# Eight batches of memory attention and routed experts on one core: loads of the first queries ahead of the keys, gate weights from GpSimd's queue, the first quarter of w1 by groups, and a new table of places

## The chip, the cores and the metric

One core of a Trainium2 chip runs the whole program. The metric is device microseconds from the start to the end of one execution. Three runs of the kernel before gave a median of 415.57 us. A separate execution was recorded by the hardware profiler; all rows below come from that one.

## What is computed

```python
# memory attention, per batch (8) and head (8); seq 576, head_dim 64, 32 memories
a = exp(phi - max(phi, axis=2)); a = a / (sum(a, axis=2) + 1e-9)      # over the 576 tokens
k_m = einsum('bhsm,bhsd->bhmd', a, k); v_m = einsum('bhsm,bhsd->bhmd', a, v)
attn = softmax(q @ k_m.T / sqrt(64)); x = attn @ v_m                  # -> (8, 576, 512)
# routed experts: 8 experts, w1 512x1024, w2 1024x512
logits = x @ w_gate; local = sigmoid(x @ w_local)
for each batch, for each token in order:
    e = argmax(logits) if first token or local < 0.5 else the token before's e
    out = softmax(logits)[e] * (relu(x @ w1[e]) @ w2[e])
```

The main part of the kernel computes, for each batch, the expert of its first token for all tokens and scales by the gate where that is the token's expert; other pairs of batch and expert that occur are added by a loop at the end (`rest`).

## The kernel before, in words

The work goes batch by batch. Per batch there are these pieces, each a function that the table `PLACES` names:

- *Memories.* `phi`, `k` and `v` are loaded (`fetch_phi`, `fetch_kv`; lines 226 to 243). The maximum over tokens is taken and spread (`f_colmax`, `f_pm`, `f_mc`, `f_pm2`, `f_cx`), subtracted, and the exponential taken (`f_sub`, `f_exp`). `f_asum` adds over tokens, `f_pkv` (line 389) is 72 small matrix products of phi with keys and values (144 instructions in the trace), in batch 0 in two pieces, of six token groups and of three; `f_sums` gives the denominators, `f_rinv` and `f_kvn` normalise, `f_pT` and `f_kvT` transpose.
- *Gate.* `f_pgg` (line 448) multiplies the memories with the gate weights `wg`, `f_ggt` copies the result to the buffer `ggt`.
- *Attention in two halves of 288 tokens*, a and z: transposed queries (`k_qT`; in batch 0 `k_q0`, products with the identity on TensorE), scores (`k_psc`), then on VectorE and ScalarE `k_turn`, `k_mx`, `k_sub`, `k_exp`, `k_sum`, `k_inv`, `k_mul`, `k_at`. The values are not multiplied in: w1 is multiplied with the memories' values instead (`w_pg`, quarter or half of the 1024 columns at a time, and `w_G`), so that G stands for w1. G and the attention are split into a high part in fp32r and the rest (`k_ah`, `k_al`; Gh, Gl).
- *The expert of the first token.* `c_pl` (line 575) gives its logits, `c_choice` (line 586) the index on VectorE, `expert` reads it into a register of SyncE. Only then can SyncE issue the loads of w1 and w2 (`load1`, `load2`), whose addresses depend on it.
- *The expert's products.* `hidden` (line 804): for tokens 0 to 255 four pairs of 128-column chunks, then for tokens 256 to 575 eight chunks, six matrix products for each chunk (Gh and Gl with the high attention, Gh with the low), evicted by ScalarE (Relu to fp32r) and VectorE (the rest). `w_split` splits w2 (ScalarE, then GpSimd). `second` and `second_turned` multiply with w2.
- *Gate of all tokens.* The `g_` steps, short VectorE instructions.

Order: `start` (line 1145) writes out by hand the head of batch 0 and parts of batch 1. Then `moe` runs batch by batch as a generator; each `yield` adds its estimated TensorE time to a clock, and every step whose place in `PLACES` is not above that clock is emitted there. A step is known by its name and its batch; a batch is 37.8 units long. The order of emission is the order on each engine's queue and on SyncE's DMA queue, where all loads and stores of this kernel stand. `warm(n)` issues n products of zeros that nothing reads.

In batch 0, tokens are handled in three blocks (`EARLY`): the first 32 tokens alone, so that the choice of the expert can be made, then 32 to 287, then 288 to 575. `fetch_q0` is a generator: its first part loads the first 32 queries (`q0e`, line 270), its second the rest (`q`, line 291, and again line 270). In `start` it is called behind the four loads of keys and values of batch 0; between its two parts stand phi of batch 1 and the two loads of gate weights (lines 190 and 191). `w_pg` for the first quarter of w1 is called as `lo`, for the second as `hi`, both in `start`, before the first product of `hidden`.

PSUM buffers: `ps_a` 3, `ps_h` 3 (hidden, quarter products, query transposes), `ps_o` 2.

## Time and profile before

| what | us |
|---|---|
| median of three runs | 415.57 |
| lowest and highest run | 414.13, 419.14 |
| profiled execution, whole | 420.2 |
| its span, first to last instruction | 418.3 |
| TensorE busy in the span | 396.8 |
| VectorE, ScalarE, GpSimd busy | 284.6, 177.8, 149.1 |

Times in the rows are microseconds from the start of the span. PE is TensorE's matrix products, PEld its weight loads, DVE VectorE, ACT ScalarE, POOL GpSimd, SP SyncE; SPq is SyncE's queue, where an entry's length is the time in which it was issued, not that of the transfer. In a timeline a row has its start, its length, the engine, the line, the operation, the tile written and read, the shape and the count; in brackets stands the idle time of the engine before it and what ended it. "issue" there means that the profile shows nothing that was waited for. The share of the DMA engines can stand a little above 1, since it counts packets that overlap.

### The profile page before, as it was taken

Reading aid. Unit: us, or ns where it says so; the run is one execution under the profiler, and the core shown is the slowest. Engines: PE = TensorE matmul, PEld = TensorE weight load, DVE = VectorE, ACT = ScalarE, POOL = GpSimd, SP = SyncE. Lnnn points to the kernel's source line nnn. Section 1 sums busy time; section 2 is a strip of 40 time slices with the busy share of each in tenths; the row PEclk is TensorE's granted clock in tenths of the full one; section 3 lists DMA queues with packets and bytes.
Section 4 is the critical chain, followed back from the end, with each engine's and each line's share of the span. In section 5 each row is a group of like instructions: output and inputs, shape, how many; then the busy total and the mean of one; then the engine's idle time right before and its main releaser. Section 6 shows DMA issues by size and latency. Waiting matters only on the chain.

```text
span 418.3 us, 10597 instructions
## 1 busy us (share of the span) xinstructions
PE 396.8 (95%) x4191; PEld 328.0 (78%) x4195; DVE 284.6 (68%) x714; ACT 177.8 (43%) x427; POOL 149.1 (36%) x160
## 2 busy tenths in 40 slices
PE   8678789999999989999999999999999999999994
PEld 2546667889787887699868997798878996899884
DVE  4476586787978698687758868588757676626300
ACT  2154633336641664525632474426541564146010
POOL 1014541426522555018610481119510670256000
PEclk9999989999999999999999999999999999999998
DMA  8879693999188966799979179884974077202011
GB/s 257 208 260 292 124 393 99 233 266 384 38 284 147 327 226 214 121 356 323 300 132 394 68 258 184 241 303 140 253 145 164 2 220 257 99 0 64 25 40 54
DMA packets 116437, 82.58 MB, mean 197 GB/s; under 512 B 70624, under 2 KB 90080, under 8 KB 116384
## 3 DMA queue, kind: packets, MB, share of 16 engines
q1 hardware_dynamic: 116384, 81.86, 66.1%
q8 instruction: 35, 0.57, 0.6%
q14 instruction: 18, 0.15, 0.1%
HBM read 66.60 MB, written 15.24 MB: 196 GB/s over the span
## 4 chain that ended last, share of the span: by engine, by line
PE 82%; DMA 6%; DVE 5%; SPq 4%; issue 1%; ACT 1%; POOL 0%; DVEq 0%
PE ph L819 20%; PE po L907 9%; PE po L857 9%; PE po L909 8%; PE po L908 8%; PE po L859 8%; PE po L858 8%; PE pkv L396 4%; PE pg L787 3%; DMA kv_t<-in_v_dram 3%; DMA out_dram<-oT 2%; PE psc L507 2%; DVE h L829 1%; DMA q<-in_q_dram 1%; PE pl L604 1%
## 5 line engine op out<-in xcount | busy, mean ns | idle before, releaser
L777 POOL TENSOR_TENSOR w2l<-raw,w2h 128x512 fp32r<-128x512 f32 x64 | 82.0, 1305 | 32.7 <-ACT w2h L776 25.1
L819 PE MATMUL ph<-ah,Gh 128*128 128x256 f32 (+1 forms) x256 | 74.5, 306 | 3.0 <-issue 1.7
L829 DVE SCALAR_TENSOR_TENSOR h<-ph,h 128x320 fp32r<-128x320 f32 (+2 forms) x104 | 52.7, 519 | 33.6 <-ACT h L827 33.2
L819 PE MATMUL ph<-ah,Gl 128*128 128x256 f32 (+1 forms) x256 | 71.7, 295 | 0.0
L907 PE MATMUL po<-h,w2l 128*128 128x320 f32 x224 | 71.5, 319 | 0.0
L909 PE MATMUL po<-h,w2h 128*128 128x320 f32 x224 | 69.2, 309 | 0.0
L908 PE MATMUL po<-h,w2h 128*128 128x320 f32 x224 | 69.2, 309 | 0.0
L827 ACT ACTIVATE h<-ph 128x320 fp32r<-128x320 f32 (+1 forms) x96 | 46.5, 490 | 46.2 <-PE ph L819 45.9
L857 PE MATMUL po<-w2h,h 128*128 128x512 f32 (+1 forms) x152 | 61.2, 403 | 0.0
L914 POOL TENSOR_TENSOR oT<-oT,gT 128x320 f32<-128x320 f32 x28 | 20.9, 745 | 106.3 <-DVE oT L913 99.4
L859 PE MATMUL po<-w2h,h 128*128 128x512 f32 (+1 forms) x152 | 58.5, 385 | 0.0
L858 PE MATMUL po<-w2l,h 128*128 128x512 f32 (+1 forms) x152 | 58.4, 384 | 0.0
L819 PEld LDWEIGHTS ph<-ah,Gh 128*128 128x128 f32 x256 | 48.1, 188 | 9.2 <-issue 5.6
L819 PE MATMUL ph<-al,Gh 128*128 128x256 f32 (+1 forms) x256 | 54.6, 295 | 0.0
L819 PEld LDWEIGHTS ph<-ah,Gl 128*128 128x128 f32 x256 | 48.2, 188 | 0.0
L907 PEld LDWEIGHTS po<-h,w2l 128*128 128x128 f32 x224 | 42.0, 188 | 5.6 <-issue 5.2
L563 POOL TENSOR_TENSOR al<-at,ah 128x576 fp32r<-128x576 f32 (+1 forms) x18 | 23.1, 1291 | 63.9 <-ACT ah L559 54.2
L776 ACT ACTIVATE w2h<-raw 128x512 fp32r<-128x512 f32 x64 | 38.3, 624 | 11.9 <-PE po L909 10.1
L908 PEld LDWEIGHTS po<-h,w2h 128*128 128x128 f32 x224 | 42.1, 188 | 0.2
L909 PEld LDWEIGHTS po<-h,w2h 128*128 128x128 f32 x224 | 42.1, 188 | 0.0
L819 PEld LDWEIGHTS ph<-al,Gh 128*128 128x128 f32 x256 | 41.0, 188 | 0.0
L857 PEld LDWEIGHTS po<-w2h,h 128*128 128x128 f32 x152 | 29.0, 191 | 14.5 <-issue 9.4
(151 smaller groups left out, 578.0 us busy)
## 6 DMA issues: line engine op xcount, KB each, us to landing
raw<-in_moe_w_dram SPq DMA_DIRECT2D x34, 512.0 KB, 5.9
raw<-in_moe_w_dram SPq DMA_DIRECT2D x15, 1024.0 KB, 5.9
kv_t<-in_k_dram SPq DMA_DIRECT2D x7, 1152.0 KB, 8.9
kv_t<-in_v_dram SPq DMA_DIRECT2D x7, 1152.0 KB, 11.3
q_t<-in_q_dram SPq DMA_DIRECT2D x112, 72.0 KB, 3.4
att_d<-at SPq DMA_DIRECT2D x8, 576.0 KB, 9.0
out_dram<-oT SPq DMA_DIRECT2D x28, 160.0 KB, 5.7
out_dram<-ot SPq DMA_DIRECT2D x17, 256.0 KB, 4.8
```

The source lines that it names most:

```text
L563: (eng or nc.gpsimd).tensor_tensor(out=st.al[:, gs, ss], in0=st.at[:, gs, ss], in1=st.ah[:, gs, ss], op=ALU.subtract)
L776: nc.scalar.activation(h, src, AF.Copy)
L777: nc.gpsimd.tensor_tensor(out=l, in0=src, in1=h, op=ALU.subtract)
L819: nc.tensor.matmul(pv[:, c - c0], lhsT=lt[:, g, cs], rhs=rt[:, g, s0 : s0 + n], start=(i == 0), stop=(i == 5),)
L827: nc.scalar.activation(hc[:, :, 0:n], pv, AF.Relu)
L829: nc.vector.scalar_tensor_tensor(out=hc[:, :, o : o + z - a], in0=pv[:, :, a:z], scalar=0.0, in1=hc[:, :, a:z], op0=ALU.max, op1=ALU.subtract,
L857: nc.tensor.matmul(po[:, c0:c1], lhsT=h[:, c, th], rhs=hi, start=(c == 0), stop=False)
L858: nc.tensor.matmul(po[:, c0:c1], lhsT=h[:, c, th], rhs=lo, start=False, stop=False)
L859: nc.tensor.matmul(po[:, c0:c1], lhsT=h[:, c, tl], rhs=hi, start=False, stop=(c == FC - 1))
L907: nc.tensor.matmul(po[:, 0:n], lhsT=lo, rhs=h[:, c, 0:n], start=(c == 0), stop=False)
L908: nc.tensor.matmul(po[:, 0:n], lhsT=hi, rhs=h[:, c, 0:n], start=False, stop=False)
L909: nc.tensor.matmul(po[:, 0:n], lhsT=hi, rhs=h[:, c, n : 2 * n], start=False, stop=(c == FC - 1))
```

## The change

In words: the first part of `fetch_q0` is called ahead of the loads of keys and values, the gate weights are issued by GpSimd, ahead of GpSimd's constants, and the rest of the queries right behind phi of batch 1. The transposes of the first 32 queries stand ahead of `f_pkv`. The warm-up of three products that stood between `f_pm` and `c_pl` stands ahead of the transposes of the second block. The values of batch 1 and the first half of w2 are named in the table instead of `start`; so are the product with the second quarter of w1 and its split, now behind the first pair of hidden chunks. The first quarter is split group by group, with the attention's high part of the same group behind it, and the first pair of hidden chunks has a PSUM buffer for each chunk and does its products with the low part last. The column sums of batch 1 move from `start` to the table, and `pkv` is three steps there. Many numbers of the table differ; the rows of it that are named in the text, and those that are new, are shown.

```diff
--- PLACES, in part
+++
-    "asum": {2: 31, 3: 64.8, 4: 92.7, 5: 128.3, 6: 165.5, 7: 203.9},
-    "pkv": {1: 1.56, 2: 34.5, 3: 67.3, 4: 93.6, 5: 128.9, 6: 166.7, 7: 204.5},
+    "v": {1: 0.02},
+    "asum": {1: 1.42, 2: 31, 3: 64.8, 4: 92.7, 5: 128.3, 6: 165.5, 7: 203.9},
+    "pkv 0": {1: 1.56, 2: 33.9, 3: 67.3, 4: 93.6, 5: 128.9, 6: 166.7, 7: 204.5},
+    "pkv 1": {1: 1.57, 2: 34.51, 3: 67.31, 4: 93.61, 5: 128.91, 6: 166.71, 7: 204.51},
+    "pkv 2": {1: 1.58, 2: 34.52, 3: 67.32, 4: 93.62, 5: 128.92, 6: 166.72, 7: 204.52},
-    "kvn": {1: 7.7, 2: 36.8, 3: 70.1, 4: 95.5, 5: 131.7, 6: 170, 7: 208.2},
+    "kvn": {1: 8.6, 2: 36.8, 3: 70.1, 4: 96.1, 5: 131.7, 6: 170, 7: 208.2},
-    "z sub": {0: 0.01, 1: 26.1, 2: 54.9, 3: 90, 4: 123, 5: 162.6, 6: 198.6, 7: 240.9},
+    "z sub": {0: 1.21, 1: 26.1, 2: 54.9, 3: 90, 4: 123, 5: 162.6, 6: 198.6, 7: 240.9},
-    "w2 0": {1: 22.7, 2: 57.9, 3: 93.2, 4: 121.1, 5: 161.2, 6: 199, 7: 235.9},
-    "pg 0": {1: 30.7, 2: 66.7, 3: 96.2, 4: 127.7, 5: 165.8, 6: 203.6, 7: 240.5},
-    "G 0": {1: 30.8, 2: 66.8, 3: 96.9, 4: 129.9, 5: 167.7, 6: 205.2, 7: 242.1},
-    "g L": {0: 6.9, 1: 30.9, 2: 62, 3: 95.2, 4: 133.4, 5: 171.2, 6: 209, 7: 248.2},
+    "w2 0": {0: 0.93, 1: 22.7, 2: 57.9, 3: 93.2, 4: 124.1, 5: 164.2, 6: 202, 7: 238.9},
+    "pg 0": {0: 0, 1: 30.7, 2: 66.7, 3: 96.2, 4: 127.7, 5: 165.8, 6: 203.6, 7: 241.1},
+    "G 0": {0: 0.01, 1: 30.8, 2: 66.8, 3: 96.9, 4: 129.9, 5: 167.7, 6: 205.2, 7: 242.7},
+    "g L": {0: 7.6, 1: 30.9, 2: 62, 3: 96.4, 4: 133.4, 5: 171.2, 6: 209, 7: 248.2},
...
@@ -187,8 +190,8 @@
             nc.gpsimd.memset(c0s[i], 0.0)
 
     def gate_weights():
-        nc.sync.dma_start(out=wg[:, :, 0:E], in_=w_gate.rearrange("(h p) e -> p h e", h=HG))
-        nc.sync.dma_start(out=wg[:, :, E : E + 1], in_=w_local.rearrange("(h p) o -> p h o", h=HG))
+        nc.gpsimd.dma_start(out=wg[:, :, 0:E], in_=w_gate.rearrange("(h p) e -> p h e", h=HG))
+        nc.gpsimd.dma_start(out=wg[:, :, E : E + 1], in_=w_local.rearrange("(h p) o -> p h o", h=HG))
 
     def pair_constants():
         nc.gpsimd.iota(pos, pattern=[[32, 2]], base=1, channel_multiplier=1, allow_small_or_imprecise_dtypes=True)
@@ -554,9 +557,9 @@
         ss = slice(32 * p[1], 32 * p[2])
         nc.vector.transpose(st.at[:, :, ss], st.sc[p[1]].rearrange("p (g i) m -> p g (i m)", g=NG))
 
-    def k_ah(st, b0, b1):
+    def k_ah(st, b0, b1, gs=slice(0, NG)):
         ss = slice(32 * b0, 32 * b1)
-        nc.scalar.activation(st.ah[:, :, ss], st.at[:, :, ss], AF.Copy)
+        nc.scalar.activation(st.ah[:, gs, ss], st.at[:, gs, ss], AF.Copy)
 
     def k_al(st, b0, b1, eng=None, gs=slice(0, NG)):
         ss = slice(32 * b0, 32 * b1)
@@ -792,16 +795,16 @@
                     stop=True,
                 )
 
-    def w_G(st, n, part=slice(0, 512)):
+    def w_G(st, n, part=slice(0, 512), gs=range(NG)):
         fs = slice(512 * n + part.start, 512 * n + part.stop)
-        for g in range(NG):
+        for g in gs:
             nc.scalar.activation(st.G[0][:, g, fs], st.pg[g][:, part], AF.Copy)
             nc.vector.tensor_tensor(
                 out=st.G[1][:, g, fs], in0=st.pg[g][:, part], in1=st.G[0][:, g, fs], op=ALU.subtract
             )
 
 
-    def hidden(G, ah, al, res, turned=False):
+    def hidden(G, ah, al, res, turned=False, apart=False):
 
         for s0, n in HALVES:
 
@@ -809,31 +812,37 @@
             res.append(ht)
             parts = ((0, n, n),) if s0 == 0 or turned else ((n - 64, n, n), (0, n - 64, n + 64))
             two = 512 // n
+            steps = [(x, ah, g) for g in range(NG) for x in G] + [(G[0], al, g) for g in range(NG)]
             for c0 in range(0, FC, two):
-                ph = ps_h.tile([P, 512], F32, tag="ph", name="ph")
-                pv = ph[:, 0 : two * n].rearrange("p (c s) -> p c s", c=two)
-                for c in range(c0, c0 + two):
-                    cs = slice(c * P, c * P + P)
-                    steps = [(x, ah, g) for g in range(NG) for x in G] + [(G[0], al, g) for g in range(NG)]
-                    for i, (lt, rt, g) in enumerate(steps):
-                        nc.tensor.matmul(
-                            pv[:, c - c0],
-                            lhsT=lt[:, g, cs],
-                            rhs=rt[:, g, s0 : s0 + n],
-                            start=(i == 0),
-                            stop=(i == 5),
+                own = apart and s0 == 0 and c0 == 0
+                phs = [ps_h.tile([P, 512], F32, tag="ph", name="ph") for _ in range(two if own else 1)]
+                each = 1 if own else two
+                pvs = [ph[:, 0 : each * n].rearrange("p (c s) -> p c s", c=each) for ph in phs]
+                for c, i in (
+                    [(c, i) for s in (range(4), range(4, 6)) for c in range(c0, c0 + two) for i in s]
+                    if own
+                    else [(c, i) for c in range(c0, c0 + two) for i in range(6)]
+                ):
+                    lt, rt, g = steps[i]
+                    nc.tensor.matmul(
+                        pvs[(c - c0) // each][:, (c - c0) % each],
+                        lhsT=lt[:, g, c * P : c * P + P],
+                        rhs=rt[:, g, s0 : s0 + n],
+                        start=(i == 0),
+                        stop=(i == 5),
+                    )
+                for k, pv in enumerate(pvs):
+                    hc = ht[:, c0 + k * each : c0 + (k + 1) * each]
+                    nc.scalar.activation(hc[:, :, 0:n], pv, AF.Relu)
+                    for a, z, o in parts:
+                        nc.vector.scalar_tensor_tensor(
+                            out=hc[:, :, o : o + z - a],
+                            in0=pv[:, :, a:z],
+                            scalar=0.0,
+                            in1=hc[:, :, a:z],
+                            op0=ALU.max,
+                            op1=ALU.subtract,
                         )
-                hc = ht[:, c0 : c0 + two]
-                nc.scalar.activation(hc[:, :, 0:n], pv, AF.Relu)
-                for a, z, o in parts:
-                    nc.vector.scalar_tensor_tensor(
-                        out=hc[:, :, o : o + z - a],
-                        in0=pv[:, :, a:z],
-                        scalar=0.0,
-                        in1=hc[:, :, a:z],
-                        op0=ALU.max,
-                        op1=ALU.subtract,
-                    )
                 yield 6 * two * (0.118 if n == 256 else 0.147)
 
     def second(ht, W2, t, gt, res, end=False, turned=False):
@@ -926,7 +935,7 @@
         b = st.b
         ht = []
         turned = b < B - 1
-        yield from hidden(st.G, st.ah, st.al, ht, turned)
+        yield from hidden(st.G, st.ah, st.al, ht, turned, b == 0)
         st.ot = {}
         for t in (0, 1) if turned else (0, 1, 4, 2, 3):
             res = []
@@ -1067,8 +1076,10 @@
         "sub 1": lambda st: f_sub(st, 1),
         "exp 0": lambda st: f_exp(st, 0),
         "exp 1": lambda st: f_exp(st, 1),
-        "asum": f_asum,
-        "pkv": f_pkv,
+        "asum": lambda st: (f_asum_tree if st.b == 1 else f_asum)(st),
+        "pkv 0": lambda st: f_pkv(st, slice(0, 3)),
+        "pkv 1": lambda st: f_pkv(st, slice(3, 6)),
+        "pkv 2": lambda st: f_pkv(st, slice(6, 9)),
         "sums": f_sums,
         "rinv": f_rinv,
         "kvn": f_kvn,
@@ -1115,8 +1126,8 @@
         "w1 1": lambda st: load1(st, 1),
         "w2 0": lambda st: load2(st, 0),
         "w2 1": lambda st: load2(st, 1),
-        "pg 0": lambda st: w_pg(st, 0),
-        "G 0": lambda st: w_G(st, 0),
+        "pg 0": lambda st: w_pg(st, 0) if st.b else w_pg(st, 0, slice(256, 512), ps_o),
+        "G 0": lambda st: w_G(st, 0) if st.b else w_G(st, 0, slice(256, 512)),
         "pg 1": lambda st: w_pg(st, 1),
         "G 1": lambda st: w_G(st, 1),
 
@@ -1145,13 +1156,13 @@
     def start():
         s, n = sts[0], sts[1]
         fetch_phi(s, True)
+        gate_weights()
         gate_constants()
+        q0 = fetch_q0()
+        next(q0)
         for i in range(2):
             fetch_kv(s, piece=PIECES[i])
-        q0 = fetch_q0()
-        next(q0)
         fetch_phi(n, False, pf, "oT")
-        gate_weights()
         next(q0)
 
         warm(11)
@@ -1161,22 +1172,22 @@
         warm(1)
         f_mc(s)
         f_pm2(s)
-        warm(14)
+        warm(12)
         f_cx(s)
         for i in range(2):
             f_sub(s, i, V)
             f_exp(s, i)
+        k_q0(s, EARLY[0])
         for i in range(2):
             f_asum_piece(s, i)
             f_pkv(s, PIECES[i])
             warm(3 * (1 - i))
         f_sums(s)
         fetch_kv(n, (0,))
-        k_q0(s, EARLY[0])
         f_rinv(s)
         f_kvn(s)
         f_colmax_tree(n, slice(0, 1))
-        warm(4)
+        warm(5)
         f_pT(s)
         warm(3)
         f_kvT(s)
@@ -1190,17 +1201,15 @@
         for f in steps:
             f(s, EARLY[0])
         p, z = EARLY[1:]
+        warm(3)
         k_q0(s, p)
         f_pm(n)
-        warm(3)
         f_mc(n)
         c_pl(s)
         c_choice(s)
         expert(s)
         load1(s, 0, 2)
         load1(s, 1)
-        fetch_kv(n, (1,))
-        load2(s, 0)
 
         k_psc(s, p)
         f_pm2(n)
@@ -1212,21 +1221,18 @@
             f(s, p)
         f_sub(n, 0, V)
         k_exp(s, p)
-        for i in range(2):
-            f_exp(n, i)
         warm(3)
         for f in steps[4:]:
             f(s, p)
-        k_ah(s, 0, PB)
-        lo, hi = slice(0, 256), slice(256, 512)
+        for i in range(2):
+            f_exp(n, i)
+        lo = slice(0, 256)
         w_pg(s, 0, lo)
+        for g in range(NG):
+            w_G(s, 0, lo, (g,))
+            k_ah(s, 0, PB, slice(g, g + 1))
         k_turn(s, z)
-        w_G(s, 0, lo)
         k_al_each(s, 0, PB)
-        f_asum_tree(n)
-        warm(1)
-        w_pg(s, 0, hi, ps_o)
-        w_G(s, 0, hi)
 
     listed = []
     with tc.manual_schedule():
```

## Rows read from the trace of the kernel before

**Rows 1.** Windows of three stages: length, busy time (instructions) by engine, clock, DMA.

```profile
0.00:31.00 31.00, 23.80 (x375) 12.97 (x387) 17.87 (x47) 10.11 (x22) 3.45 (x28) 1.00 0.81 241
31.00:60.00 29.00, 22.17 (x345) 17.81 (x332) 20.48 (x59) 14.88 (x37) 14.03 (x15) 1.00 0.93 258
60.00:420.00 360.00, 350.84 (x3480) 297.19 (x3479) 246.27 (x610) 152.83 (x368) 131.61 (x119) 0.99 0.63 188
```

**Rows 2.** The chain of waits of the first 36 us: start, length, what.

```profile
14.05 5.53 DMA q<-in_q_dram
...
24.74 0.41 SPq L755
...
26.59 10.89 DMA kv_t<-in_v_dram
```

**Rows 3.** Timeline of TensorE, 30 to 60 us.

```profile
30.83 0.67 PE L787 MATMUL pg<-raw,kvT 64*32 64x256 f32 x16 [1.15 <-DMA raw<-in_moe_w_dram]
31.43 0.38 PE L819 MATMUL ph<-ah,Gh 128*128 128x256 f32 x1
...
34.51 1.09 PE L787 MATMUL pg<-raw,kvT 64*32 64x512 f32 x16 [1.40 <-DMA raw<-in_moe_w_dram]
...
37.61 2.24 PE L396 MATMUL pkv<-kv_t,phi_t 64*32 64x128 f32 x144 [0.39 <-DMA kv_t<-in_v_dram]
...
43.80 0.39 PE L819 MATMUL ph<-ah,Gh 128*128 128x256 f32 x1 [1.72 <-issue]
...
59.18 0.69 PE L507 MATMUL psc<-qT,kvT 64*32 64x288 f32 x8 [1.93 <-DVE qT L480]
```

**Rows 4.** Windows as in rows 1; the last three numbers are clock, DMA share, GB/s.

```profile
4.00:6.00 2.00, 1.87 (x5) 0.47 (x4) 1.87 (x2) 0.00 (x0) 0.00 (x0) 1.00 0.81 251
6.00:13.00 7.00, 5.09 (x93) 2.65 (x101) 3.42 (x7) 1.54 (x3) 0.00 (x0) 1.00 1.07 328
13.00:15.00 2.00, 1.60 (x76) 0.98 (x64) 0.00 (x0) 0.00 (x0) 0.00 (x0) 1.00 0.57 118
...
26.00:38.00 12.00, 8.28 (x120) 4.56 (x125) 8.91 (x18) 6.54 (x15) 4.44 (x6) 1.00 1.00 346
60.00:63.00 3.00, 3.00 (x8) 2.38 (x8) 2.42 (x5) 0.61 (x2) 1.31 (x2) 0.53 1.05 403
```

**Rows 5.** Timeline of TensorE, 14 to 23 us.

```profile
14.57 0.91 PE L396 MATMUL pkv<-kv_t,phi_t 64*32 64x128 f32 x47 [0.24 <-DMA kv_t<-in_v_dram]
...
18.47 0.28 PE L453 MATMUL pgg<-wg,kvT 64*32 64x9 f32 x16
19.72 1.97 PE L496 MATMUL pq<-ident,q 128*64 128x128 f32 x32 [0.97 <-DMA q<-in_q_dram]
...
22.00 0.59 PE L305 MATMUL wp<-wz 128*128 128x512 bf16 x2
22.52 0.24 PE L578 MATMUL pl<-ggt,at 128*1 128x8 f32 x4
```

**Rows 6.** Timeline of VectorE, 20 to 23 us.

```profile
20.63 0.25 DVE L555 STREAM_TRANSPOSE at<-sc 128x64 f32<-128x64 f32 x1
21.98 0.29 DVE L350 TENSOR_REDUCE mc<-pm 128x2 f32<-128x128 f32 x1 [1.11 <-PE pm L346]
22.81 0.15 DVE L591 TENSOR_REDUCE m<-pl 1x1 f32<-1x8 f32 x1 [0.53 <-PE pl L578]
```

**Rows 7.** Timeline of SyncE's queue, 4 to 13 us.

```profile
4.07 4.55 SPq L270 DMA_DIRECT2D q0e<-in_q_dram x2
...
9.14 2.29 SPq L190 DMA_DIRECT2D wg<-in_moe_w_gate_dram x1
11.47 1.38 SPq L191 DMA_DIRECT2D wg<-in_moe_w_local_dram x1
```

**Rows 8.** Timeline of TensorE, a wait at 152 us.

```profile
152.39 0.41 PE L819 MATMUL ph<-ah,Gh 128*128 128x320 f32 x1 [1.32 <-DVE h L829]
```

16 lines of the change are left out of this document (8 added, 8 removed), and 102 rows, old and new, of the table PLACES.

## The prediction

> **What bounds the kernel now.** I read the page first, then a table by stage, then the chain of waits of the start, the timelines of TensorE, VectorE and SyncE's queue there, and last what the DMA engines moved.
>
> The stages differ [rows 1]. From 60 us on TensorE is busy 350.84 of the 358.3 us that are left of the span: the reader is to see that nothing but TensorE's own work counts there, apart from the last stores. Before 60 us it has gaps: 23.80 of 31 us busy, part of that warm-up products that compute nothing, and then 22.17 of 29. All that the change edits by hand lies in these first 60 us.
>
> The chain of waits says what the first stage hangs on [rows 2]: two loads of the first queries that end at 14.05 + 5.53 = 19.58, the choice of the first expert, the load of w1 that SyncE can only issue at 24.74 because its address is the chosen expert, and the values of batch 1, issued behind w1 at 26.59 and landed at 37.48. TensorE's `pkv` products of batch 1 begin right there, at 37.61 [rows 3], with the quarter products of w1 before them waiting for their own loads (1.15 at 30.83 and 1.40 at 34.51). Between 26 and 38 us the DMA engines are full (share 1.00, 346 GB/s) [rows 4]. So the first stage is worth exactly what the choice is worth: if the w1 loads go out x us earlier, everything to 37.6 moves by x, and nothing else in that stretch can move it.
>
> **The change part by part.**
>
> *Order on TensorE around the choice.* `pgg` ends at 18.47 + 0.28 = 18.75. Then TensorE waits 0.97 for the queries, transposes them from 19.72, does `pm`, a warm-up of three products (0.52 from 22.00 to the next), and only then `pl` at 22.52 [rows 5]. What `pl` reads, the first block of attention, was ready at 20.63 + 0.25 = 20.88 on VectorE [rows 6], 1.64 earlier. The change puts the warm-up ahead of the transposes and takes it out behind `pm`. From the start of the transposes to `pl` it is now 22.52 − 19.72 − 0.52 = 2.28. With warm-up from 18.75 to about 19.4 (two products took 0.59), `pl` comes at 19.4 + 2.28 = 21.68, that is 0.84 earlier, still behind the 20.88. VectorE's `mc` follows `pm` and takes 0.29; it began 2.26 after the transposes began, so it would run from 21.66 to 21.95, and `m` began 0.29 after `pl`, which gives 21.97: both fit. I take 0.8 us.
>
> *That needs the queries by 19.4.* They landed at 19.58. On SyncE's queue the two gate weight loads held 2.29 and 1.38 us, 3.67 together, in front of them [rows 7]; these leave that queue. The long 4.55 at `q0e` is not its own price: it stands behind the keys there and waits for room; as the third and fourth load it is short. The queries so come up to 3.7 earlier, and need 0.2: this step has a margin. If the queries came no earlier, the transposes would start at 19.72 still, and the gain would be 0.5.
>
> *What goes ahead of the keys and values.* The last value piece of batch 0 lets `pkv` start at 14.57 after a wait for the DMA [rows 5], and from there to `pgg` the work follows step by step; a later landing by d shifts `pgg` and the choice by d. Two things now come in front: `q0e` (64 KB), and the gate weights (18 KB in rows of 32 and 4 bytes) on GpSimd's queue. No run shows a DMA on that queue. From 13 to 15 us, the stretch in which the gate weights' loads were due, the DMA engines moved only 118 GB/s at share 0.57, against 328 GB/s at 1.07 from 6 to 13 [rows 4]. Counted by busy share: 1.14 us of engine time for 236 KB, of which that many bytes cost 0.77 at the rate of the stretch before, so 0.37 for the small rows. Counted by lost bytes: 2 × (328 − 118) = 420 KB, which is 1.28 us. `q0e` at 64 KB is 0.2 at 328 GB/s, and 0.5 at the poor rate. On the other side, from 4 to 6 us the engines stand at share 0.81, 0.38 us free, which may swallow all of it. Lower bound of d: 0 (an earlier landing has no reason, since nothing is taken away in front of the keys). Upper bound: 1.28 + 0.5 = 1.8. I take 0.37 + 0.2 − 0.2 (half of the free time) = 0.35, near the count by share, because another queue can use the engines while the small rows leave them idle. The choice is then 0.8 − 0.35 = 0.45 us earlier.
>
> The Trainium skill, "DMA: Bandwidth & Descriptors", section "Issuing engines are not separate DMA queues", speaks against more: loads from GpSimd's queue run on the same 16 engines and only SyncE's issue time is saved. By that rule the small rows cost what they cost in any queue, only now in front of the keys, and the sum would be that of the second rival; the share of 0.57 is why I don't take it whole.
>
> *GpSimd.* Its constants now stand behind two DMA issues. The first that is read is the gate product's buffer after `pgg` at 18.75. Were generating a load as slow as SyncE's slowest here, 4.55 for two [rows 7], they would still be done ten microseconds before. Nothing, as long as that cover holds; every microsecond past 18.75 would be a microsecond on the choice.
>
> *The transposes of the first block ahead of `pkv`, fewer warm-up products there.* TensorE waits for the values at this point anyway. Nothing.
>
> *First quarter of w1 by groups, first hidden pair apart, second quarter's product moved into the loop.* In the kernel before, the second quarter's 0.67 of products, after a wait of 1.15, stand in front of the first hidden pair at 31.43 [rows 3]. Now the pair goes first. But the pair is followed by `pg 1`, which waits until 34.51 for the second half of w1, and then by `pkv`, which waits for the values. So about a microsecond that the pair gains becomes a longer wait at 34.51: its wait grows from 1.40 to about 2.2. The extra evictions of the pair lie in that same wait. The scores of the second half on VectorE now stand behind the second quarter's split and, in the table, behind that of `G 1`, which waits for the same load; what is late next is the second half's attention, used after 43.8. Bounds: 1.15 + 0.67 = 1.8 gained if the wait at 34.51 were not there, 1.3 lost if the softmax steps are late by one batch of such instructions. I take nothing.
>
> *v of batch 1 and w2 moved into the loop.* On SyncE the order stays: three w1 loads, v, w2, queries. The wait behind each is the same. Nothing.
>
> *Column sums of batch 1 later on GpSimd, `pkv` in three parts.* The parts stand directly behind one another for all batches but 2, where the first goes one step ahead. Same instructions, same order. Nothing.
>
> *The new table.* Worked through the yields, most numbers fall on the same step; some 70 steps move, most by one, `w2 0` of batches 4 to 7 by three or four steps later, `z qT 1` of these by three or more earlier. In a stage that TensorE fills to 98% [rows 1] they can only cost or win single waits, such as the one of 1.32 at 152.39 [rows 8]. I take nothing, with 1.3 to both sides.
>
> *Sum.* The profiled execution: 420.2 − 0.45 = 419.75. Its time stands 4.6 above the median of the runs; the same 0.45 off 415.57 gives 415.1. The runs before lie between 414.13 and 419.14, and 2% of the time, 8.3 us, is about what a measurement of this kernel can tell from no change; the forecast is far inside.
>
> **The rivals.** First, *more is won after 37 us*. TensorE stands 1.72 us at 42.08 for no reason that the profile shows, and 1.93 at 59.18 for a transpose on VectorE [rows 3]; after the latter the granted clock is 0.53 from 60 to 63 (most of that at 1.2 GHz), a loss of 3 × 0.47 = 1.4 us [rows 4]. If the earlier hidden pair lets VectorE run ahead, the first gap can close and the clock stay at 2.4 GHz: 415.57 − 0.45 − 1.72 − 1.4 = 412.0. For it: GpSimd and ScalarE get the first pair's work a microsecond sooner. Against it: the first gap has no releaser among the engines, and VectorE is full before 59 us, with the same steps in the same order.
>
> Second, *the keys are late* (slower). The gate weights and `q0e` take their full lost-bytes price in front of the keys, d = 1.8: `pkv`, `pgg`, the choice, w1 and the values of batch 1 are 1.8 − 0.8 = 1.0 later: 416.6. It decides from d = 0.8 on. For it: the drop to 118 GB/s. Against it: the engines' idle share in both stretches.
>
> Third, *the table hurts*: one wait of 1.3 in each of batches 4 to 7 (w2 late or VectorE's early transposes in front of evictions): 415.1 + 5.3 = 420.4. Against it: loads with a whole batch of slack, and a stage that shows one such wait in all.
>
> That the change does not do what it says, because `pl` is held by something else than the warm-up and the queries, gives 415.6 to 415.9; it can't be told from the forecast by the time.
>
> **How the numbers follow.** Forecast 0.55, first rival 0.22, second 0.17, third 0.06. The range runs from the first rival, 411.8, to 417.7, a microsecond past the second, for the spread of the medians; it leaves out the third and the tails. Faster by over 2% would need more than all gaps of 31 to 60 us together, 6.8, and something beyond: 0.03. Slower by over 2%: only the third rival with more on top, 0.03. Within 2%: 0.94.
>
> **What would show it.** In the profile after: no wait of the `pq` transposes for the queries; `pl` near 22.1; the first w1 issue near 24.3; `pkv` of batch 1 near 37.2; the last value piece of batch 0 landing 0.3 to 0.4 later, so `pkv` near 14.9; the wait before `pg 1` longer than 1.40; TensorE's total busy time the same. Wrong would be: `pkv` of batch 0 after 15.4 (second rival), a first w1 issue unmoved, the gap at 42 us gone and the clock full at 60 us (first rival), or new waits after 140 us (third).

## The result and the profile after

| | us |
|---|---|
| kernel after, median of 20 runs (lowest to highest) | 418.37 (416.23 to 420.21) |
| kernel before, median of 20 runs (lowest to highest) | 416.15 (414.13 to 419.14) |
| ratio of after to before, 95% interval | 1.0042 (1.0022 to 1.0061) |
| profiled execution of after, its span | 418.31, 416.5 |

The change makes the kernel slower by 0.42%, that is 1.75 us (0.9 to 2.5). The forecast was 0.45 faster, with a range up to 417.7; the time lies outside it, and the sign is wrong. The change is small against the 2% that the forecast names, but the interval of the ratio leaves out 1, so it is a loss.

The pair of profiled executions says the opposite: 420.2 before, 418.31 after. The profiled execution of before was slower than all of its 20 plain runs. The forecast was made on that one execution, and the experiments show that this is a large part of what went wrong.

Windows of the kernel after: length, busy time (instructions) of TensorE, its weight loads, VectorE, ScalarE, GpSimd, then clock, DMA share, GB/s. They answer to [rows 1, 4].

```profile
0.00:31.00 31.00, 24.62 (x379) 13.64 (x379) 18.25 (x47) 10.31 (x23) 6.15 (x32) 1.00 0.84 261
31.00:60.00 29.00, 24.57 (x342) 18.88 (x343) 23.55 (x63) 14.91 (x39) 14.33 (x14) 0.94 0.93 275
60.00:420.00 360.00, 348.32 (x3475) 295.07 (x3473) 243.98 (x606) 152.49 (x368) 129.19 (x117) 0.99 0.62 185
...
4.00:6.00 2.00, 1.62 (x5) 0.42 (x3) 2.00 (x2) 0.00 (x0) 0.40 (x7) 1.00 0.86 205
6.00:13.00 7.00, 5.27 (x114) 3.05 (x118) 3.46 (x8) 1.81 (x4) 0.00 (x0) 1.00 1.03 332
13.00:15.00 2.00, 1.95 (x90) 1.17 (x73) 0.00 (x0) 0.00 (x0) 0.00 (x0) 1.00 1.13 337
26.00:38.00 12.00, 9.54 (x236) 6.00 (x221) 8.84 (x18) 6.50 (x16) 4.44 (x6) 1.00 1.07 354
```

From 60 us on the span holds 356.5 us, of which TensorE is busy 348.32: the late stage has not changed its nature. From 4 to 6 us the DMA engines are busier than before (share 0.86 against 0.81) and move less (205 against 251 GB/s). From 13 to 15 us, where the gate weights used to stand, they now move 337 in place of 118. The poor stretch behind the keys is gone, and one stands in front of them.

TensorE in the timeline of the kernel after, answering to [rows 3, 5, 8]:

```profile
11.74 1.58 PE L399 MATMUL pkv<-kv_t,phi_t 64*32 64x128 f32 x96 [1.37 <-DMA kv_t<-in_v_dram]
...
14.13 0.91 PE L399 MATMUL pkv<-kv_t,phi_t 64*32 64x128 f32 x47
...
17.20 0.40 PE L510 MATMUL psc<-qT,kvT 64*32 64x32 f32 x14
18.18 0.22 PE L510 MATMUL psc<-qT,kvT 64*32 64x32 f32 x2 [0.58 <-issue]
18.30 0.28 PE L456 MATMUL pgg<-wg,kvT 64*32 64x9 f32 x16
18.51 0.82 PE L308 MATMUL wp<-wz 128*128 128x512 bf16 x3
19.26 1.97 PE L499 MATMUL pq<-ident,q 128*64 128x128 f32 x32
21.16 0.33 PE L349 MATMUL pm<-ident,cm 128*128 128x128 f32 x1
21.42 0.25 PE L581 MATMUL pl<-ggt,at 128*1 128x8 f32 x4
...
27.56 0.67 PE L790 MATMUL pg<-raw,kvT 64*32 64x256 f32 x16 [0.47 <-DMA raw<-in_moe_w_dram]
29.30 0.39 PE L827 MATMUL ph<-ah,Gh 128*128 128x256 f32 x1 [1.06 <-ACT ah L562]
32.77 1.09 PE L790 MATMUL pg<-raw,kvT 64*32 64x512 f32 x16 [0.61 <-DMA raw<-in_moe_w_dram]
35.68 2.25 PE L399 MATMUL pkv<-kv_t,phi_t 64*32 64x128 f32 x144 [0.21 <-DMA kv_t<-in_v_dram]
...
56.23 1.19 PE L510 MATMUL psc<-qT,kvT 64*32 64x288 f32 x8 [1.94 <-DVE qT L483]
149.49 0.41 PE L827 MATMUL ph<-ah,Gh 128*128 128x320 f32 x1 [1.32 <-DVE h L838]
```

The queries are no longer waited for: `pq` stands right behind the warm-up at 19.26. What the chain now hangs on is `pkv`, its first piece waiting 1.37 for the values, then a gap of 0.58 that waits for nothing the profile shows, among the scores, two products short of `pgg`.

Set against the one profile of before, the signs that the forecast named for the choice came out earlier than it asked: `pl` at 21.42 (22.1 was forecast), `pkv` of batch 1 at 35.68 (37.2), and the first issue of w1, in the rows below, at 23.65 (24.3). The kernel is slower all the same, so the comparison with that profile misleads.

SyncE's queue and GpSimd's two loads in the timeline of the kernel after, answering to [rows 2, 7]:

```profile
1.75 0.93 SPq L273 DMA_DIRECT2D q0e<-in_q_dram  x2
2.72 0.43 SPq L234 DMA_DIRECT2D kv_t<-in_k_dram  x1
...
6.81 7.38 SPq L294 DMA_DIRECT2D q<-in_q_dram  x4
...
23.65 1.56 SPq L758 DMA_DIRECT2D raw<-in_moe_w_dram  x3
...
1.34 0.92 POOL L193 DMA_DIRECT2D wg<-in_moe_w_gate_dram  x1 [0.32 <-issue]
2.59 0.78 POOL L194 DMA_DIRECT2D wg<-in_moe_w_local_dram  x1
```

GpSimd's issuing took 0.92 and 0.78 us, more than ten microseconds before `pgg` at 18.30, behind which the first of GpSimd's constants is read. `q0e` takes 0.93 to issue as the third and fourth load in place of 4.55.

VectorE in the timeline of the kernel after, answering to [rows 6]:

```profile
20.40 0.24 DVE L558 STREAM_TRANSPOSE at<-sc 128x64 f32<-128x64 f32 x1
21.53 0.29 DVE L353 TENSOR_REDUCE mc<-pm 128x2 f32<-128x128 f32 x1 [0.88 <-PE pm L349]
21.73 0.14 DVE L594 TENSOR_REDUCE m<-pl 1x1 f32<-1x8 f32 x1
```

`m` follows `mc` without a wait, as worked out, and 0.31 behind `pl`.

### The profile page after: what moved, and what is told of

The parts are those of the page before. It is cut to its first block, busy times and chain, and to the rows that moved or that the text cites. A ratio compares the mean times of both kernels' runs of the same rounds, so it can differ in the third digit from the quotient of the medians.

```text
span 416.5 us, 10603 instructions
## 1 busy us (share of the span) xinstructions
PE 397.5 (95%) x4193; PEld 327.6 (79%) x4193; DVE 285.8 (69%) x715; ACT 177.7 (43%) x429; POOL 149.7 (36%) x162
## 4 chain that ended last, share of the span: by engine, by line
PE 62%; DVE 0%; issue 0%; ACT 0%
PE ph L827 16%; PE po L866 7%; PE po L868 6%; PE po L867 6%; PE po L916 6%; PE po L917 6%; PE po L918 6%; PE pg L790 2%; PE pkv L399 2%; PE psc L510 1%; PE po L890 1%; PE pl L607 1%; PE pm L358 0%; PE pT L438 0%; PE pgg L456 0%; DVE at L558 0%
## 5 line engine op out<-in xcount | busy, mean ns | idle before, releaser
L836 ACT ACTIVATE h<-ph 128x320 fp32r<-128x320 f32 (+2 forms) x97 | 46.5, 485 | 45.0 <-PE ph L827 44.9
```

Of the source, the lines that this page charges most:

```text
L836: nc.scalar.activation(hc[:, :, 0:n], pv, AF.Relu)
```

## The experiments

Eighteen runs were made, e1 to e18; some repeat a kernel, and e6, e7 and e12 are told of without a row. The table holds what the text draws on, from the profile of each, which is one execution: GB/s from 5 to 7 us; the start of the second piece of `pkv` in batch 0; the gap marked "issue" just before `pgg`; the time from `pgg` to `pl`; the first issue of w1; the start of `pkv` of batch 1. A ratio is to the kernel before.

| kernel | ratio (95%) | GB/s 5 to 7 | pkv, 2nd piece | gap | pgg to pl | w1 issue | pkv, batch 1 |
|---|---|---|---|---|---|---|---|
| before, as shown ahead | | 313 | 14.57 | 0.29 | 4.05 | 24.74 | 37.61 |
| e1 before again | 1.0008 (0.9974, 1.0043) | 320 | 13.54 | 0 | 3.38 | 22.54 | 36.51 |
| e4 before, new table | 1.0008 (0.9981, 1.0036) | 303 | 13.68 | 0 | 3.01 | 22.28 | 34.72 |
| after | 1.0042 (1.0022, 1.0061) | 240 | 14.13 | 0.58 | 3.12 | 23.65 | 35.68 |
| e2 after again | 1.0058 (1.0015, 1.0100) | 229 | 14.06 | 1.40 | 3.12 | 24.41 | 36.80 |
| e3 after, old table | 1.0036 (0.9992, 1.0080) | 231 | 14.32 | 0.22 | 3.11 | 23.48 | 36.08 |
| e16 after, no moved warm-up | 1.0030 (1.0001, 1.0059) | 230 | 13.76 | 1.40 | 2.49 | 23.44 | 36.42 |
| e13 after, another warm-up out | 1.0063 (1.0034, 1.0092) | 222 | 13.96 | 1.12 | 3.11 | 24.04 | 37.30 |
| e8 before, loads of after | 1.0014 (0.9982, 1.0046) | 262 | 13.99 | 1.27 | 3.01 | 24.09 | 38.04 |
| e5 gate loads back | 0.9993 (0.9964, 1.0023) | 381 | 12.71 | 0.30 | 3.38 | 22.21 | 35.98 |
| e15 the same again | 0.9987 (0.9957, 1.0017) | 375 | 13.42 | 0 | 3.12 | 22.14 | 35.37 |
| e17 e5, no moved warm-up | 0.9984 (0.9956, 1.0012) | 370 | 12.72 | 0 | 3.18 | 21.68 | 33.84 |
| e14 e5, another warm-up out | 1.0006 (0.9978, 1.0034) | 373 | 12.54 | 0 | 3.30 | 21.43 | 34.70 |
| e9 after, no gate loads | 0.9996 (0.9974, 1.0017) | 365 | 13.27 | 0.46 | 3.12 | 22.57 | 35.40 |
| e10 queries split | 1.0033 (1.0000, 1.0066) | 359 | 13.53 | 0 | 3.11 | 22.71 | 34.58 |
| e11 e10, no moved warm-up | 0.9978 (0.9959, 0.9997) | 369 | 12.78 | 1.40 | 3.97 | 24.25 | 36.59 |
| e18 e11 again | 1.0011 (0.9977, 1.0045) | 386 | 12.52 | 1.56 | 2.48 | 22.38 | 35.11 |

**Both kernels again.** No edit; the same two kernels, each with another profile.

> The kernel before, unchanged, profiled a second time. Its first profile took 420.2 us, above every one of its 20 plain times (414.13 to 419.14). Theory A, the profile was an unlucky execution: now 414 to 417 us, and one or both of the two oddities of the first 65 us are gone, the gap of 1.72 at 42 us without a releaser and the half clock from 60 to 63.5 us. Theory B, the profile is typical of profiled executions: again about 420 us with both. Ratio to itself 1.000 within 0.003.

> The changed kernel, unchanged, profiled a second time, beside the kernel before on the same chip. Theory A and B alike: about 418.3 us and a ratio of 1.004. What is asked is whether the half clock that its first profile shows from 56 to 59.7 us, behind a wait of 1.94, stands in each execution: if so it costs some 1.7 us in each.

The times held: 1.0008 and 1.0058. What did not hold is the start of the kernel before. The timeline of e1, TensorE and SyncE's queue:

```profile
13.54 0.91 PE L396 MATMUL pkv<-kv_t,phi_t 64*32 64x128 f32 x47 [0.50 <-DMA kv_t<-in_v_dram]
...
17.51 1.97 PE L496 MATMUL pq<-ident,q 128*64 128x128 f32 x32 [0.31 <-DMA q<-in_q_dram]
20.31 0.24 PE L578 MATMUL pl<-ggt,at 128*1 128x8 f32 x4
...
22.54 1.56 SPq L755 DMA_DIRECT2D raw<-in_moe_w_dram  x3
```

The wait for the queries is 0.31, not 0.97, and w1 goes out 2.2 us earlier than in the execution the forecast was built on. e4, whose start is that of before, agrees:

```profile
17.25 1.97 PE L496 MATMUL pq<-ident,q 128*64 128x128 f32 x32
...
22.28 1.56 SPq L755 DMA_DIRECT2D raw<-in_moe_w_dram  x3
```

Against these two, the first issue of w1 is late by 0.9 to 2.1 in the five profiles with the start of after (after, e2, e3, e13, e16), which fits the sign of the plain runs.

e1's profile, at 419.07 us, answers neither of its two theories: the start was early, the whole time long. Part of that is TensorE's clock. From 26 to 38 us e1 shows

```profile
26.00:38.00 12.00, 9.89 (x181) 6.39 (x186) 6.57 (x13) 4.27 (x10) 4.42 (x6) 0.72 1.03 323
```

where the kernel after has a granted clock of 1.00 (row above). The half clock that e2 asks about does not stand in each execution. It stands from 56 to 60 us in the kernel after, behind the wait of 1.94; near 31 to 35 and 58 to 62 in e2; near 27 to 34 and 57 to 62 in e1; nowhere in the first 65 us of e5, e15, e16 and e17. It doesn't separate before from after: the mean granted clock of the plain runs is 0.993 in both (20 runs of after; 135 of before beside the experiments).

**The table.** One row of the pattern, after with the numbers of before where both tables know the step (e3), and before with the new ones (e4):

```diff
-    "kvn": {1: 8.6, 2: 36.8, 3: 70.1, 4: 96.1, 5: 131.7, 6: 170, 7: 208.2},
+    "kvn": {1: 7.7, 2: 36.8, 3: 70.1, 4: 95.5, 5: 131.7, 6: 170, 7: 208.2},
```

> The changed kernel with the old numbers in the table (only the entries that the change adds are kept, pkv in three steps at the old place). Theory T, the new table costs the time: ratio 0.995 to 0.999, since the start alone would win 0.5 to 2 us. Theory S, the start costs the time although its first loads go out earlier: ratio 1.003 to 1.006 as for the whole change.

> The kernel before with the new numbers in the table, the start unchanged (pkv in one step). Theory T: ratio 1.004 to 1.008, the whole loss or more. Theory S: 0.998 to 1.002.

1.0036 with the old numbers, 1.0008 for the new numbers alone: the table is worth nothing that these runs resolve, and the loss stays with the start.

**Gate loads back on SyncE's queue,** behind phi of batch 1, the first queries still ahead of the keys.

```diff
-        nc.gpsimd.dma_start(out=wg[:, :, 0:E], ...)
+        nc.sync.dma_start(out=wg[:, :, 0:E], ...)
...
         fetch_phi(s, True)
-        gate_weights()
         gate_constants()
...
         fetch_phi(n, False, pf, "oT")
+        gate_weights()
         next(q0)
```

> The changed kernel with the two gate weight loads back on SyncE's queue, behind phi of batch 1 and ahead of the rest of the queries; q0e stays ahead of the keys. Theory K, the small rows taken between 4 and 7 us delay keys and values by 0.5 to 1 us: the second pkv piece is back at 13.5 to 13.8 (14.1 to 14.3 in three profiles with the change's loads). Theory F, TensorE's next block of instructions (one packet of the instruction queue) waits in the DMA engines behind data issued earlier than before, and pgg starts 2.5 us after that packet: the packet is back at 13 to 13.8 us, no gap in front of pgg, pl at 20.1 to 20.6 and not 21.2 to 22.2. Both: ratio 0.998 to 1.002. Theory C, the order of TensorE's own work in the start costs the time: ratio 1.003 to 1.006 as before.

> The kernel with the gate weights back on SyncE's queue once more, in the same call as the two without the warm-up: 0.9975 to 1.001 if its first result holds. Above 1.002 would mean that the gate loads alone don't explain the loss of the kernel after.

0.9993, and 0.9987 when repeated: the loss is gone both times. The second piece of `pkv` starts at 12.71 and 13.42, earlier than the 13.5 to 13.8 that was expected. The stretch from 5 to 7 us, first of the kernel after, then of e5:

```profile
5.00:7.00 2.00, 1.26 (x7) 0.40 (x7) 1.33 (x3) 0.00 (x0) 0.00 (x0) 1.00 0.97 240
```

```profile
5.00:7.00 2.00, 0.80 (x5) 0.30 (x6) 1.32 (x2) 0.00 (x0) 0.00 (x0) 1.00 1.05 381
```

The engines are as full in the one as in the other, and move 141 GB/s less: 18 KB in small rows take the place of 2 × 141 = 282 KB of keys and values, 0.7 us at 381 GB/s. All six rows of the table with the gate loads in front stand at 222 to 262 GB/s there; the eight without them, and with the first queries ahead of the keys, stand at 359 to 386.

**No gate loads at all.** The gate weights are filled with a constant, so the choice of experts is left out of the work (the first expert everywhere).

```diff
-        nc.gpsimd.dma_start(out=wg[:, :, 0:E], ...)
-        nc.gpsimd.dma_start(out=wg[:, :, E : E + 1], ...)
+        nc.gpsimd.memset(wg, 0.01)
```

> The changed kernel without the two gate weight loads: the tile is filled with a constant by GpSimd, so every batch takes expert 0 and the gate is not the reference's; all else is as changed, the queries issued as early as there. Theory K (the small rows in front of keys and values are the cost): the second pkv piece at 12.6 to 12.9 as in e5_gate_back, 14.1 to 14.3 in the changed kernel. Theory F (the instruction packet waits behind queries issued early): the packet comes 3 to 4 us after pkv has begun, as in the changed kernel, not 2 to 3, and a gap of 0.5 to 1.4 us stands in front of pgg although keys and values are early. Without F no gap over 0.3. Time: ratio 0.993 to 0.998 if both loads and queue are free.

0.9996: with the loads gone, all else of the change in place, the loss is gone too. That is the second way to the same reading, though not the full gain that was expected (0.993 to 0.998). The second piece of `pkv`, at 13.27, came later than the 12.6 to 12.9 of theory K, and the gap of 0.46 lies between what theory F asked for (0.5 or more) and what its absence did (0.3 at most).

**First queries back behind the keys** (e6), and with the gate loads back as well (e7):

```diff
-        q0 = fetch_q0()
-        next(q0)
         for i in range(2):
             fetch_kv(s, piece=PIECES[i])
+        q0 = fetch_q0()
+        next(q0)
```

> The changed kernel with q0e issued behind the keys and values as before, the gate weights still on GpSimd's queue. Theories K and F: the loss stays, ratio 1.002 to 1.006, pl after 21. If the 64 KB of q0e ahead of the keys were the cost: ratio 1.000, second pkv piece at 13.6.

> The changed kernel with all loads of the start in the order and on the queue of the kernel before; the order of the compute steps, the first hidden pair and the table as changed. Theories K and F: no loss, ratio 0.997 to 1.001, w1 issued at 22.3 to 22.8. Theory C: 1.003 to 1.006.

Both are far slower, 1.0140 (1.0099 to 1.0180) and 1.0113 (1.0070 to 1.0156), and for one reason. TensorE in the timeline of e6:

```profile
14.77 0.60 PE L496 MATMUL pq<-ident,q0e 32*128 32x32 f32 x4 [4.76 <-DMA q0e<-in_q_dram]
```

The transposes of the first queries now stand ahead of `pkv` on TensorE, so the whole queue waits 4.76 for them (4.32 in e7). Part of the loss is the clock behind that wait: it was granted at half from 14 to 18 us in e6, and the first `pkv` piece takes 2.81 there in place of 1.58. The two edits of the change are a pair: the move on TensorE needs the move of the load. These two say nothing of the gate loads.

**The loads alone** in the kernel before:

```diff
         fetch_phi(s, True)
+        gate_weights()
         gate_constants()
+        q0 = fetch_q0()
+        next(q0)
         for i in range(2):
             fetch_kv(s, piece=PIECES[i])
-        q0 = fetch_q0()
-        next(q0)
         fetch_phi(n, False, pf, "oT")
-        gate_weights()
         next(q0)
```

> The kernel before with only the loads of the start as changed (q0e ahead of the keys, gate weights from GpSimd's queue). Theories K and F: the whole loss or more, ratio 1.004 to 1.007, w1 issued at 23.4 to 24.4, an instruction packet after 15 us. Theory C: 0.998 to 1.001.

1.0014 (0.9982 to 1.0046) holds both no loss and the whole of it: inconclusive in time, and under the 1.004 that theories K and F asked for. Its profile has the late start, w1 at 24.09.

**Gate loads elsewhere.** Between the second and the third block's queries (e10, on top of e5), the same without the moved warm-up (e11, e18), and on ScalarE's queue behind the exponentials (e12):

```diff
# e10, fetch_q0 and start
+            if c == 0:
+                yield
...
         next(q0)
+        gate_weights()
+        next(q0)
# e11 and e18 besides
         p, z = EARLY[1:]
-        warm(3)
         k_q0(s, p)
# e12
+        nc.scalar.dma_start(out=wg[:, :, 0:E], ...)
```

> e5_gate_back (gate weights on SyncE's queue) with the two loads of the second block's queries ahead of the gate weights and the two of the third block behind them. The queries that the choice waits for should be there before 17 us, so that pl comes 0.2 to 0.3 earlier than the 19.98 there, held then by the three warm-up products ahead of the transposes; w1 issued at 21.9 to 22.1. Theory F: keys, phi and queries lie more densely in front of the instruction packet, which may take that back with a gap in front of pgg. Ratio 0.996 to 1.001.

> e10_queries_split without the three warm-up products ahead of the transposes of the second block. pl is then held by the first block's attention alone: 19.1 to 19.5, w1 issued at 21.3 to 21.8, and everything to pkv of batch 1 earlier by 0.6 us than in e5_gate_back. Ratio 0.994 to 0.999; if a half clock follows from the missing warm-up, 0.5 to 1.7 us are lost again.

> The kernel of the faster result (gate weights between the second and third block's queries on SyncE's queue, no warm-up ahead of the transposes) once more. If its 0.9978 holds, 0.996 to 0.9995 again; if the order of the queries decides nothing, it agrees with the kernel with the gate weights back and without this warm-up within 0.001.

> The changed kernel with the gate weights issued from ScalarE's queue behind the two exponentials (at about 10 us) instead of GpSimd's at 1.3 us. Theory K: the small rows then share the engines with the last of the values and phi of batch 1; the second pkv piece at 12.7 to 13.6. Theory F: the queries are issued as early as in the changed kernel, so the gap in front of pgg stays at 0.5 to 1.4. Ratio 0.998 to 1.003.

e10 gave 1.0033, above e5 though its keys are not as late as in the kernel after; the intervals overlap. Its profile (416.38 us, where the median of its runs is 418.65) shows no gap and w1 at 22.71, so where e10 loses stays open. e11 gave 0.9978 and seemed to beat both kernels; repeated as e18 it gave 1.0011, so that gain is not confirmed. (The 3.97 of e11's profile is the clock: it was granted at 0.57 from 18 to 22 us, behind the gap of 1.40, and the transposes took 3.56 us in place of 1.97; those of e18 did not.) e12 lost 1.0128 (1.0092 to 1.0164). TensorE in its timeline:

```profile
19.61 0.28 PE L456 MATMUL pgg<-wg,kvT 64*32 64x9 f32 x16 [2.28 <-DMA wg<-in_moe_w_local_dram]
```

ScalarE issued the loads at 12.81 and 14.35 only, and `pgg` waits 2.28 for them; the transposes behind it took 3.60 us in place of 1.97, at a granted clock of 0.66 from 20 to 25 us.

**The moved warm-up.** The expectations of e13 and e14 speak of the three products of zeros ahead of `k_q0(s, p)`; their edit took out those ahead of the first quarter product instead, behind `k_exp(s, p)`. e16 and e17 made the edit that was meant.

```diff
# e13 (of after) and e14 (of e5)
         k_exp(s, p)
-        warm(3)
         for f in steps[4:]:
# e16 (of after) and e17 (of e5)
         p, z = EARLY[1:]
-        warm(3)
         k_q0(s, p)
```

> The kernel after without the three products of zeros ahead of the transposes of the second block. If the moved warm-up costs the choice what it takes on TensorE (three products, about 0.9 us where the queries have already landed), this is 0.5 to 1.0 us faster than the kernel after: 1.0015 to 1.003 of the kernel before, and the stretch from pgg to pl in its profile is under 2.9 us. If all of the loss comes from what stands ahead of the keys, it stays at 1.004 +- 0.001 and pgg to pl at 3.1.

> Gate weights back on SyncE's queue behind phi of batch 1, first queries still ahead of the keys, and without the three products of zeros ahead of the transposes of the second block. If the gate loads and the moved warm-up are two costs that add, this is 0.998 or less of the kernel before (0.9993 less 0.6 to 0.9 us), as the kernel with split queries and no warm-up was. If the warm-up costs nothing, 0.9993 +- 0.001 as with the warm-up.

> The kernel after without the three products of zeros ahead of the transposes of the second block, and with all other warm-up left in (the two runs before took out the three products ahead of the first quarter product instead). If the moved warm-up costs the choice what it takes, 0.75 us on TensorE from 18.51 to 19.26 of the profile after, and this goes through to the end, the ratio is 1.0015 to 1.003, and pgg to pl is 2.3 to 2.6 where the transposes run at 2.4 GHz. If the softmax on VectorE sets the choice then (attention ready 2.1 after pgg), or the transposes run at 1.2 GHz for want of work before them, it stays at 1.003 to 1.006.

> Gate weights back on SyncE's queue behind phi of batch 1, first queries still ahead of the keys, and without the three products of zeros ahead of the transposes of the second block alone. If gate loads and moved warm-up are two costs that add, 0.9975 or less of the kernel before. If the warm-up is worth nothing, 0.999 +- 0.001 as with it.

e13 and e14 gave 1.0063 and 1.0006: no gain in either. e13 and e14 differ from each other by the gate loads' queue and place alone, and so do e16 and e17, and each pair ran side by side. The means of the pairs lie 2.6 us (95%: 1.9 to 3.3) and 1.8 us (0.8 to 2.8) apart, the kernel with the gate loads in front slower both times. TensorE of e16, then of e17:

```profile
18.63 0.22 PE L510 MATMUL psc<-qT,kvT 64*32 64x32 f32 x2 [1.40 <-issue]
18.75 0.28 PE L456 MATMUL pgg<-wg,kvT 64*32 64x9 f32 x16
18.96 1.97 PE L499 MATMUL pq<-ident,q 128*64 128x128 f32 x32
...
21.24 0.24 PE L581 MATMUL pl<-ggt,at 128*1 128x8 f32 x4
```

```profile
16.27 0.28 PE L456 MATMUL pgg<-wg,kvT 64*32 64x9 f32 x16
17.30 1.97 PE L499 MATMUL pq<-ident,q 128*64 128x128 f32 x32 [0.75 <-DMA q<-in_q_dram]
...
19.45 0.24 PE L581 MATMUL pl<-ggt,at 128*1 128x8 f32 x4
```

With the queries landed early (e16), taking out the warm-up shortens `pgg` to `pl` from 3.12 to 2.49, that is 0.63; so there it is a cost on the path. With the queries late again (e17), a wait of 0.75 stands in its place, and 3.18 is no shorter: there it is free. In time the gain is within the noise (1.0030 against 1.0042).

**The gap in front of `pgg`.** A packet of the queue named "instruction" explains where it ends. The DMA view of a quarter microsecond, 15.5 to 15.75 of the kernel after, then 15.0 to 15.25 of e18:

```profile
q8 instruction: 1, 0.02, 29.9%
```

```profile
q8 instruction: 1, 0.02, 29.9%
```

And TensorE in the timeline of e18:

```profile
12.52 0.94 PE L401 MATMUL pkv<-kv_t,phi_t 64*32 64x128 f32 x48
...
15.59 0.40 PE L512 MATMUL psc<-qT,kvT 64*32 64x32 f32 x14
17.55 0.22 PE L512 MATMUL psc<-qT,kvT 64*32 64x32 f32 x2 [1.56 <-issue]
17.69 0.28 PE L458 MATMUL pgg<-wg,kvT 64*32 64x9 f32 x16
```

TensorE resumes 2.68 after the start of that quarter in the one and 2.55 in the other. In the twelve profiles with such a gap (before, after, e2, e3, e5, e8, e9, e11, e12, e13, e16, e18) this lies between 2.55 and 2.80, while the gap itself runs from 0.22 to 1.56; in e4 the packet lies at 13.0 to 13.25, 3.5 ahead of the scores at 16.77, and there is no gap. The other profiles bear this out: in the twelve with a gap the scores begin 0.59 to 2.14 us after the start of the packet's quarter, and in the eight without one (e1, e4, e6, e7, e10, e14, e15, e17) 2.35 to 4.50 us after it. So the gap reads as TensorE waiting for its own instructions; the trace does not say for which engine a packet is. e18 shows what this is worth: its keys are the earliest of all, and 1.56 of that is given back here.

## Why the prediction was wrong

*The baseline.* "They landed at 19.58", "w1 ... at 24.74": both are rows of one execution, the latest of the three profiles of that start. Its time stood 4.6 above the median, which the forecast noted and then passed over by taking the difference off the median. A gain that consists in taking away a wait holds only as far as the wait is there in the ordinary execution; the 0.97 for the queries is 0.31 and 0 in the two other profiles of that start.

*Order on TensorE, 0.8 us gained: this step failed.* The working itself holds: `pq` to `pl` is 21.42 − 19.26 = 2.16 (2.28 was forecast) and the warm-up ends at 19.26 (19.4). But from `pgg` to `pl` the kernel after needs 3.12, and e1 and e4 need 3.38 and 3.01, so it gains 0.26 on the one and loses 0.11 on the other, where the 4.05 of the one profile had promised 0.93. Where the queries are not late, the warm-up has merely changed its place on the path. e16 shows that the gain could have been had without it: 2.49.

*The queries by 19.4: right,* with the margin as said.

*What goes ahead of the keys, 0.35: near in sum by luck, wrong in its parts; this is the second step that failed.* (As written, 0.37 + 0.2 − 0.2 is 0.37.) Against e1 and e4 (mean 13.61) the second piece of `pkv` starts at 14.05 in the mean of after, e2, e3, e13 and e16: 0.44 later. But the parts are larger and of opposite sign: with the gate loads back, e5, e14, e15 and e17 start it at 12.85 in the mean (12.71, 12.54, 13.42, 12.72). So the gate loads cost 1.2 there, near the count by lost bytes (1.28), not the 0.37 of the count by share; and the rest, 0.76 earlier, goes to the first queries ahead of the keys, which were to cost 0.2. (TensorE's order differs there too, so 0.76 is not theirs alone by any run.) That they help the engines has a row: e7, which differs from e5 by the place of the first queries alone, moves 317 GB/s from 5 to 7 us, e5 381. (The nearness to 1.28 is partly luck: with the same loads, e1 and e4 move 209 and 207 GB/s from 13 to 15 us, not 118, and the same count gives 0.7 there.) The bound "an earlier landing has no reason" was the mistake here. The rule of the Trainium skill, "DMA: Bandwidth & Descriptors", section "Issuing engines are not separate DMA queues", that the queue which issues a load does not spare the engines its transfer, was the better guide: the trace agrees, 240 GB/s where e5, with the same loads further back, has 381.

*A term that was missing.* The gap in front of `pgg` stood in the trace of before (0.29) and not in the sum. It is 0.22 to 1.40 in the five profiles of the start of after (mean 0.94) and none in e1 and e4. Together: 0.44 later keys, 0.94 of gap, and nothing from the order on TensorE make 1.4; the first issue of w1 is later by 23.90 − 22.41 = 1.49 (after, e2, e3 and e13 against e1 and e4), and the time by 1.75 (0.9 to 2.5). This is against e1 and e4; with the first profile of before taken in, the issue is later by only 0.7 in the mean. The step from there on, "if the w1 loads go out x us earlier, everything to 37.6 moves by x", holds only roughly: from the first issue of w1 to `pkv` of batch 1 the table has 11.87 to 13.97 us. With the gate loads in front (after, e2, e3, e13, e16) the two stand at 23.80 and 36.46 in the mean, with them back (e5, e14, e15, e17) at 21.87 and 34.97, so 1.9 at the issue is 1.5 at `pkv`.

*The second rival came true in part.* Its sign and its mechanism, small rows that delay the keys, are what the runs show. But it asked for d = 1.8 and a `pkv` after 15.4, and 0.44 and 14.13 came; it was to decide from d = 0.8 on, and decided at 0.44, because the 0.8 on the other side was not there. That its 1.0 us (416.6) lies inside the measured 0.9 to 2.5 is luck: much of the delay is the gap, which no rival names. *The first rival* did not: no gap of 1.72 is seen at 41 us (0.47), but e1 has none either without the change, and the wait of 1.94 for VectorE at 56.23 is still there, with half clock behind it. (Its sum gives 412.0; the range starts at 411.8.) *The third rival* did not: e3 and e4.

*GpSimd, first quarter by groups, v and w2 moved, column sums and `pkv` in parts, the table, all at nothing:* right as far as runs show. e5, e15 and e9 hold all of these edits (but for GpSimd's loads) and lie within 0.13% of before, each with an interval of 0.2 to 0.3% to either side; that holds for their sum, not for each. The wait at the second quarter did not grow to 2.2 in the kernel after (0.61 at 32.77), where 1.06 of waiting for ScalarE stands ahead of the pair, at 29.30; in e5, with its earlier issue of w1, it is 2.16, as worked out.

So the failed steps are a gain taken from a wait of one execution (0.8 forecast; +0.26 and −0.11 against e1 and e4) and the price of the gate loads in front of the keys (0.37 taken, 1.2 measured at `pkv`, with the gap on top). That the gate loads' place makes the loss is shown in time by e5, e15 and e9 and by the two pairs. What stays open: how the 1.75 is shared between the landing of the keys and the late instruction packet, and why e10, with no gate loads in front of the keys, stood at 1.0033. Every kernel that puts the gate loads in front also issues the 1 MB of queries right behind phi. e9 and e12, which do only the second, had gaps of 0.46 and 0.41; e10, e11 and e18, which issue the first half of the queries there, 0, 1.40 and 1.56. That the packet waits behind the queries' data fits this, and is not shown. No kernel that ran beats the kernel before in a way that a repeat confirms; the best are those with the gate loads back, three runs at 0.9984 to 0.9993.

## What to carry to other kernels

Take more than one profile before pricing a wait of a microsecond in the start of a kernel: here the three profiles with the start of before put the same issue at 22.28, 22.54 and 24.74, and the forecast took off a wait that is mostly absent. A load of a few KB in very short rows can cost the engines what a far larger one costs: here 18 KB in rows of 4 and 32 bytes took the place of 282 KB. An idle issuing queue did not make it cheap; its place here is behind the loads that are waited for first, but not so late that its own reader waits (2.28 in e12). When a load is moved and a consumer is moved with it, test each alone: here the consumer without the load cost 1.1 to 1.4%.

## What was not expected of the hardware

TensorE seems to stand for its own instructions at times: gaps of 0.22 to 1.56 us marked "issue", each ending 2.55 to 2.80 us after the start of the quarter microsecond that holds a packet of an instruction queue (35 such packets carry 0.57 MB in the kernel after, 16 KB each), in a stretch in which the DMA engines are full (share 1.13 from 13 to 15 us in the kernel after). And loads on GpSimd's queue are cheap to issue (0.92 and 0.78 us for 512 rows each in a kernel's first three microseconds) while the same loads held SyncE's queue for 2.29 and 1.38 [rows 7]: here the issue time tells where a load stands in a full queue, not what it costs the engines.
